# A window-attention and feed-forward kernel: score matmuls of the first two batches on tiles of 64 rows by 32 columns, and the second batch's value products in pieces of 32 moving columns

## The chip, the cores and the metric

The kernel runs on one core of one Trainium2 chip. The metric is the device time of one execution in microseconds (us): 975.45 us in the median of two runs (975.3 and 975.6). A profile of one execution lies beside it; its span is the time from the first to the last instruction.

The engines of a core are named in the profile as PE (TensorE matmul), PEld (its weight loads), DVE (VectorE), ACT (ScalarE), POOL (GpSimd) and SP (SyncE, which issues the DMAs).

## The reference

Eight batches, eight heads, 512 local and 32 global positions, head size 64. Local queries see the 32 global keys and the local keys within 32 positions; global queries see everything. The result goes through a feed-forward block.

```python
k_all = np.concatenate([k_g, k_l], axis=2)
s_g = scale * np.matmul(q_g, k_all.transpose(0, 1, 3, 2))
out_g = np.matmul(sm(s_g), v_all)
s_ll = np.where(np.abs(pos[:, None] - pos[None, :]) <= 32, scale * q_l @ k_l.T, -1e9)
s_lg = scale * np.matmul(q_l, k_g.transpose(0, 1, 3, 2))
a_l = sm(np.concatenate([s_lg, s_ll], axis=-1))
out_l = np.matmul(a_l, np.concatenate([v_g, v_l], axis=2))
x = np.concatenate([out_g, out_l], axis=2)  # to (4352 tokens, 512)
h = x @ w_in          # 512 -> 2048
y = (h - np.tanh(h)) @ w_out
```

(Lines shortened; `sm` is the softmax, `scale` is 1/8.)

## The kernel before

**Heads and pairs.** Two heads of a batch make a `Pair`: the even head lies in partitions 0 to 63 (`a.e` = 0), the odd one in 64 to 127 (`a.e` = 64). Four pairs make a batch. The 512 local queries of a head are four blocks of 128, taken two at a time (`tp` = 0, 1); a pair is thus visited twice for its scores, twice for its transposes and twice for its products.

**Scores** (`Pair.scores`, matmul on L1149). For a visit, each of the two heads has one PSUM bank with two blocks of scores. One matmul takes 64 rows (the head's 64 partitions), a stationary operand of 128 queries and a moving operand of `KC` = 224 keys. In the first two batches (`split` is false) the operands are plain fp32 and a visit is four matmuls: two blocks by two heads. In the later batches (`split` is true) the operands are split in a high and a low part (fp32r) and a visit is 12 matmuls. One plain fp32 matmul of the program shows in the trace as two weight loads and two matmuls; so a visit of the first two batches is 8 matmuls in the trace.

**After the scores** DVE adds the mask and takes the maximum (L1458), ACT the exponential (L1465), DVE the inverse sum (L1221, L1222), POOL normalises (L1228), PE transposes the probabilities (`Pair.transposes`, L1170: 16 matmuls of 64 rows and up to 128 stationary columns, moving 64), and ACT or DVE copy them to `keys_first` (L869).

**Products** (`Pair.add_product`, matmul on L1247). The stationary operand is 64 columns of values (128 or 96 rows), the moving one 160, 128, 96 or 64 columns of `keys_first`; the even head writes PSUM partitions 0 to 63, the odd one 64 to 127. `PARTS` has four parts for each of the two products of a pair, and their moving widths add up to 512 columns. So a product is 4 parts by 2 heads, 8 matmuls in the program and 16 in the trace, in every batch. Copies to `x_hi` (L869) and `x_lo` (L1258) follow.

**Feed-forward.** `Chunk.add_hidden` (L1520, input weights) and `Chunk.add_out` (L1568, output weights) run with one batch's delay: 128x512 matmuls of fp32r in three passes. Those of batch 0 begin near 58 us and share PE with the attention of batch 1.

**Fill.** Before 72 us of the planner's clock, dummy matmuls on a mask (L1814) are put where the planner sees PE waiting.

**Order.** Nothing is scheduled on the chip. `Order.run` is a planner in the kernel's own code: each operation has a due time, an engine and an estimated length (`d`; 0.85 for a plain score visit, 1.05 for a product of the first two batches), and the planner writes out one fixed order for each engine. PSUM banks 0 to 3 are handed round among scores, transposes and products; 4 to 7 hold the output sums. A score visit's two banks are free again once DVE has read them.

Of the kernel before, what the change touches and what calls it, by code (L numbers as in the profile page):

```python
# [16 lines left out]
P = 128  # L17
D = 64
KC = 224
# [4 lines left out]
def f32(ap):  # L24
    return ap.bitcast(F32)


def view(ap, dims, off=0):

    return bass.AP(ap.tensor, ap.offset + off, [list(ap.ap[0])] + [list(d) for d in dims])  # L30
# [19 lines left out]
class Order:  # L50
# [14 lines left out]
    def add(self, eng, fn, due, r=(), w=(), res=(), alloc=(), free=(), lat=0.0, xfer=0.0, rows=1.0, ldw=0.107, tail=0.107, lock=False, mode="f", glue=None):  # L65
        o = Op()
        engs = [x + (0.0,) * (3 - len(x)) + (lock,) * (len(x) < 4) for x in (eng if isinstance(eng, list) else [eng])]
        o.eng = {x[0]: x[1:3] for x in engs}

        o.lock = {x[0] for x in engs if x[3] or x[0] == "P"}  # L70
        o.xfer, o.rows, o.ldw, o.tail, o.mode = xfer, rows, ldw, tail, mode
        o.fn, o.due, o.lat, o.alloc, o.free = fn, due, lat, alloc, free
        o.n, o.ready, o.succ, o.start, o.args, o.seq = 0, 0.0, {}, None, {}, len(self.ops)
        before = {}
        for k in tuple(r) + tuple(w) + tuple(res):
            if k in self.writer:
                before[id(self.writer[k])] = self.writer[k]
        for k in tuple(w) + tuple(res):
            for x in self.readers.get(k, ()):
                before[id(x)] = x  # L80
        for x in before.values():
            x.succ[id(o)] = o
            o.n += 1
        for k in r:
            self.readers.setdefault(k, []).append(o)
        for k in w:
            self.writer[k] = o
            self.readers[k] = []
        o.next = None
        if glue is not None:  # L90
            glue.next, o.args = o, glue.args
        self.ops.append(o)
        return o
# [111 lines left out]
def kernel(ctx, tc, q_l, k_l, v_l, q_g, k_g, v_g, w_in, w_out, out):  # L205
    nc = tc.nc
# [45 lines left out]
    first_kw = cp.tile([P, 2, 2 * S], F32, name="first_kw", tag="x_lo1")  # L252
    first_kw = [first_kw[:, 0, :2 * KG], first_kw[:, 1, :2 * KG], first_kw2]
    first_q = cp.tile([P, 4 * DM], F32, name="first_q", tag="w_out_lo4")
    wide = [wpair, first_q[:, 2 * DM:].rearrange("p (n k) -> p n k", k=2), stage[:, 0], stage[:, 1]]
    first_q = [first_q[:, :S], first_q[:, S:2 * S], cp.tile([P, S], F32, name="first_q2", tag="hi0")]
    first_q = [x.rearrange("p (t c) -> p t c", t=NT) for x in first_q]
    keys_first = cp.tile([P, 2, 2, 2, 384], F32, name="keys_first", tag="kf")
    values = cp.tile([P, 2, 6, D], F32, name="values")
# [21 lines left out]
    def activations(b):  # L281
        return [t[0] if b % 2 == 0 else t[1]() for t in (x_hi, x_lo)]
# [10 lines left out]
    def bank(shape, j, dt=F32):  # L293
        n = 1
        for d in shape[1:]:
            n *= d
        t = banks[j][:shape[0], :n].bitcast(dt)
        if len(shape) == 3:
            t = t.rearrange("p (a c) -> p a c", a=shape[1])
        elif len(shape) == 4:  # L300
            t = t.rearrange("p (a c e) -> p a c e", a=shape[1], c=shape[2])
        return t
# [7 lines left out]
               step=102.1945, step1=21.2806, lag0=117.1894, hs0=56.6249, tol=0.0795, xs=0.0659, xw=9.5452, o_ld0=-439.2206,  # L310
# [557 lines left out]
    def copy(e, dst, src):  # L868
        (nc.scalar.copy if e == "A" else nc.vector.tensor_copy)(dst, src)  # L869

    def either(n, kind, psum=False):

        a, d = CFG.get("a_" + kind, 0.0), CFG.get("d_" + kind, CFG["pen"] if psum else 0.0)
        if psum:
            return [("A", (n + 190) / 1200, a), ("D", (n + 151) / 960, d)]
        return [("D", (n / 2 + 148) / 960, d, True), ("A", (n + 230) / 1200, a)]
# [95 lines left out]
    def keys_of(x, t):  # L972
        c = t // 2 * KG + t % 2 * P
        return x[:, c:c + KC]
# [33 lines left out]
    class Pair:  # L1008
# [123 lines left out]
        def scores(self, tp):  # L1132
            names = [(f"s{tp}", a.i) for a in self.heads]
            split = self.b > 1

            def mm(e, tags):
                t_ = [bank([P, 2, 256], tags[n]) for n in names]
                for a, x in zip(self.heads, t_):
                    setattr(a, f"s_{tp}", x)
                passes = [(0, 0), (0, 1), (1, 0)] if split else [(0, 0)]  # L1140
                for i in range(2):
                    for n, (qi, ki) in enumerate(passes):
                        for a, x in zip(self.heads, t_):
                            r, t = slice(a.e, a.e + D), 2 * tp + i
                            if split:
                                q, k = q_parts[qi]()[r, t * P:(t + 1) * P], keys_of(kw_parts[ki](), t)[r]
                            else:
                                q, k = first_q[self.set][r, t], keys_of(first_kw[self.set], t)[r]
                            nc.tensor.matmul(x[:, i, :KC], q, k, start=n == 0, stop=n == len(passes) - 1)  # L1149

            return dict(fn=mm, d=0.76 if split else 0.85, names=names, r=["kw0", "kl0", "kg0", "hk0", "lq"] if split else self.key[2:],
                        res=[a.p(tp) for a in self.heads], rows=0.8 if split else 1.0, ldw=0.107, tail=0.093 if split else 0.187)
# [83 lines left out]
        def add_product(self, pair):  # L1236
            o = ("o", self.j, pair, "p")
            cc, cols = self.jj, slice(256 * pair, 256 * pair + 256)
            x = [("x", self.b % 2, a.h, pair) for a in self.heads]
            over = [f"{n}{u}" for n in ("rk", "rq", "pw", "pk") for u in range(2)] if self.b == 1 else []  # L1240
            box = {}

            def mm(e, tags):
                box["o"] = bank([P, 288], tags[o])
                for i, (a, t, k, (c0, c1), o0) in enumerate(PARTS[pair]):
                    for h in self.heads:
                        nc.tensor.matmul(box["o"][h.e:h.e + D, o0:o0 + c1 - c0], values[:k, h.two, t + t // 2 + a], keys_first[:k, h.two, pair, a, c0:c1],  # L1247
                                         start=i == 0, stop=i == 3, skip_group_check=True)

            def places():  # L1250
                return [t[:, cc, cols].rearrange("p (t c) -> p t c", c=P) for t in activations(self.b)]

            def high(e, _):
                copy(e, places()[0], view(box["o"], [(160, 2), (1, P)]))

            def rest(e, _):
                src, g = box["o"], view(xg[:, cc, self.b // NG * P + self.b % NG:B * G], [(NG, G)])
                nc.vector.tensor_sub(places()[1], view(src, [(160, 2), (1, P)]), f32(places()[0]))  # L1258
                if pair:
                    nc.vector.tensor_add(g, src[:, P:P + G], g)  # L1260
                else:
                    nc.vector.tensor_copy(g, src[:, P:P + G])

            due = self.due(self.C["o_pv"] + self.C["o_pvp"] * pair)
            reads = [f"h{pair}0", f"h{pair}1", "hg0", "hg1", "vh0", "vh1"]
            add(("T", 0.92 if self.b > 1 else 1.05), mm, due, r=reads, w=[o], res=[k + (0,) for k in x] + over, alloc=[(o, self.tag)], rows=1.0,
                ldw=0.053, tail=0.135, mode="c")
            add(either(256, "ph", True), high, due + 0.5, r=[o], w=[k + (0,) for k in x])
            add(("D", 0.6), rest, due + 1, r=[o] + [k + (0,) for k in x],
                w=[k + (1,) for k in x] + [y for a in self.heads for y in (("xg", a.i, pair), ("xgw", a.i))], free=[(o, 1)])  # L1270
# [483 lines left out]
    for i in range(NH):  # L1754
# [6 lines left out]
        b, h = i // H, i % H  # L1761
# [89 lines left out]
```

## Time and profile before

| | before |
|---|---|
| time, median of 2 runs | 975.45 us (975.3 to 975.6) |
| span of the profiled execution | 973.7 us |
| PE busy | 960.3 us (99%) |
| DVE busy | 580.3 us (60%) |
| ACT busy | 452.1 us (46%) |
| POOL busy | 387.3 us (40%) |
| granted TensorE clock, mean | 1.000 |

Busy times of PE are those of pipelined matmuls with modelled ends: neighbouring matmuls overlap, so the pace of a block is read from start to start and not from the mean duration of one.

### The profile page before, as it was taken

Reading aid. Unit: us, or ns where it says so; the run is one execution under the profiler, and the core shown is the slowest. Engines: PE = TensorE matmul, PEld = TensorE weight load, DVE = VectorE, ACT = ScalarE, POOL = GpSimd, SP = SyncE. Lnnn points to the kernel's source line nnn. Section 1 sums busy time; section 2 is a strip of 40 time slices with the busy share of each in tenths; the row PEclk is TensorE's granted clock in tenths of the full one; section 3 lists DMA queues with packets and bytes.
Section 4 is the critical chain, followed back from the end, with each engine's and each line's share of the span. In section 5 each row is a group of like instructions: output and inputs, shape, how many; then the busy total and the mean of one; then the engine's idle time right before and its main releaser. Section 6 shows DMA issues by size and latency. Waiting matters only on the chain.

```text
span 973.7 us, 18494 instructions
## 1 busy us (share of the span) xinstructions
PE 960.3 (99%) x6453; PEld 784.5 (81%) x6453; DVE 580.3 (60%) x1907; ACT 452.1 (46%) x1275; POOL 387.3 (40%) x526
## 2 busy tenths in 40 slices
PE   8899999999999999999999999999999999999998
PEld 5677877888888888888888888888888888888897
DVE  6997667766657555766676567657636544422211
ACT  6966575745455434654355444534535434111111
POOL 4666756534444433434234444333332332211221
PEclk9999999999999999999999999999999999999999
DMA  8565244321223121322123122221202200100010
GB/s 233 151 178 165 84 114 114 92 38 35 50 39 82 33 39 34 88 40 34 32 38 83 23 39 39 71 50 34 50 14 69 39 17 1 44 1 1 1 44 22
DMA packets 195166, 57.32 MB, mean 59 GB/s; under 512 B 179712, under 2 KB 188416, under 8 KB 195072
## 3 DMA queue, kind: packets, MB, share of 16 engines
q1 hardware_dynamic: 193728, 55.61, 24.1%
q8 instruction: 51, 0.84, 0.4%
q10 hardware_dynamic: 1344, 0.52, 0.2%
q14 instruction: 43, 0.35, 0.1%
HBM read 47.19 MB, written 8.91 MB: 58 GB/s over the span
## 4 chain that ended last, share of the span: by engine, by line
PE 93%; DVE 2%; ACT 2%; SPq 1%; issue 1%; DMA 1%; POOL 0%; POOLq 0%; DVEq 0%; ACTq 0%
PE bank L1520 39%; PE bank L1568 38%; PE bank L1247 6%; PE bank L1149 4%; PE bank L1170 4%; PE bank L1339 1%; SPq L1030 0%; PE bank L1046 0%; DMA wraw<-in_q_g_dram 0%; ACT t L1465 0%; ACT pg L1090 0%; POOL prob L1228 0%; DVE keys_first L869 0%; ACT prob L1465 0%; ACT keys_first L869 0%
## 5 line engine op out<-in xcount | busy, mean ns | idle before, releaser
L1537 POOL TENSOR_TENSOR glo<-t,ghi 128x512 fp32r<-128x512 f32 x107 | 139.1, 1301 | 328.9 <-PE bank L1568 130.0
L1528 ACT ACTIVATE t<-bank 128x512 f32<-128x512 f32 x136 | 81.3, 598 | 302.7 <-PE bank L1520 292.3
L1531 DVE TENSOR_TENSOR t<-bank,t 128x512 f32<-128x512 f32 x136 | 93.9, 691 | 202.5 <-ACT t L1528 201.8
L1228 POOL TENSOR_SCALAR prob<-prob,st 128x224 f32<-128x224 f32 x240 | 108.0, 468 | 143.3 <-DVE st L1222 124.9
L1568 PE MATMUL bank<-w_out_hi,ghi 128*128 128x512 f32 x544 | 152.7, 394 | 0.0
L1568 PE MATMUL bank<-w_out_hi,glo 128*128 128x512 f32 x544 | 151.5, 392 | 0.0
L1568 PE MATMUL bank<-w_out_lo,ghi 128*128 128x512 f32 x544 | 151.3, 392 | 0.0
L1520 PE MATMUL bank<-x_hi,w_in_hi 128*128 128x512 f32 x512 | 140.3, 397 | 0.3 <-DVE x_hi L869 0.3
L1520 PE MATMUL bank<-x_lo,w_in_hi 128*128 128x512 f32 x512 | 137.4, 390 | 0.0
L1520 PE MATMUL bank<-x_hi,w_in_lo 128*128 128x512 f32 x512 | 136.2, 390 | 0.0
L1465 ACT ACTIVATE prob<-prob,st 128x224 f32<-128x224 f32 x240 | 113.2, 475 | 14.9 <-DVE st L1458 13.7
L1458 DVE CUSTOM_DVE_ANT_0 prob<-bank,mask 128x224 f32<-128x224 f32 x240 | 80.8, 386 | 64.7 <-PE bank L1149 57.8
L1568 PEld LDWEIGHTS bank<-w_out_lo,ghi 128*128 128x128 f32 x544 | 101.1, 188 | 22.1 <-issue 1.0
L1568 PEld LDWEIGHTS bank<-w_out_hi,glo 128*128 128x128 f32 x544 | 101.0, 188 | 21.9 <-issue 0.7
L1568 PEld LDWEIGHTS bank<-w_out_hi,ghi 128*128 128x128 f32 x544 | 100.2, 188 | 22.2 <-issue 1.4
L1520 PEld LDWEIGHTS bank<-x_hi,w_in_hi 128*128 128x128 f32 x512 | 93.7, 188 | 24.7 <-issue 3.2
L1520 PEld LDWEIGHTS bank<-x_lo,w_in_hi 128*128 128x128 f32 x512 | 95.9, 188 | 20.2
L1520 PEld LDWEIGHTS bank<-x_hi,w_in_lo 128*128 128x128 f32 x512 | 95.7, 188 | 19.7
L869 ACT COPY keys_first<-bank 128x512 f32<-128x512 f32 (+2 forms) x150 | 69.9, 516 | 89.2 <-PE bank L1170 88.3
L1247 PE MATMUL bank<-keys_first,values 128*64 128x160 f32 (+3 forms) x1024 | 68.7, 276 | 2.2 <-DVE keys_first L869 1.1
L1247 PEld LDWEIGHTS bank<-keys_first,values 96*64 96x64 f32 (+1 forms) x1024 | 56.3, 136 | 9.5 <-ACT keys_first L869 2.9
L1381 DVE STREAM_TRANSPOSE gt<-pg 32x128 f32<-32x128 f32 x192 | 53.1, 276 | 10.2 <-POOL pg L1360 4.3
(164 smaller groups left out, 1222.9 us busy)
## 6 DMA issues: line engine op xcount, KB each, us to landing
values<-in_v_l_dram SPq DMA_DIRECT2D x128, 72.0 KB, 2.2
out_dram<-wpair SPq DMA_DIRECT2D x32, 256.0 KB, 2.0
rawkq<-in_k_l_dram SPq DMA_DIRECT2D x96, 64.0 KB, 2.3
rawkq<-in_q_l_dram SPq DMA_DIRECT2D x96, 64.0 KB, 2.2
values<-in_v_g_dram SPq DMA_DIRECT2D x64, 48.0 KB, 2.0
first_q<-in_moe_w_in_dram SPq DMA_DIRECT2D x6, 512.0 KB, 4.5
stage<-in_moe_w_out_dram SPq DMA_DIRECT2D x6, 512.0 KB, 4.0
stage<-in_moe_w_in_dram SPq DMA_DIRECT2D x6, 512.0 KB, 4.0
```

The lines of the kernel that those rows point to most:

```text
L869: (nc.scalar.copy if e == "A" else nc.vector.tensor_copy)(dst, src)
L1149: nc.tensor.matmul(x[:, i, :KC], q, k, start=n == 0, stop=n == len(passes) - 1)
L1228: nc.gpsimd.tensor_scalar(x, x, st[:, c:c + 1], 1.0, op0=ALU.mult, op1=ALU.mult)
L1247: nc.tensor.matmul(box["o"][h.e:h.e + D, o0:o0 + c1 - c0], values[:k, h.two, t + t // 2 + a], keys_first[:k, h.two, pair, a, c0:c1], start ...
L1381: nc.vector.transpose(gt[r, :c], view(src, [(P, c), (1, 32)], 32 * q))
L1458: nc.vector.tensor_tensor_reduce(out=self.pt(2 * tp + i)[:, :KC], in0=getattr(self, f"s_{tp}")[:, i, :KC], in1=masks[2 * tp + i], scale=-0 ...
L1465: nc.scalar.activation(x, x, AF.Exp, bias=col[:, c0 + i:c0 + i + 1], scale=-1.0, accum_out=col[:, 8 + tp + c0 + i:9 + tp + c0 + i])
L1520: nc.tensor.matmul(self.h[s][:, j * n:(j + 1) * n], w[:, cc, f * P:(f + 1) * P], self.x()[xi][:, cc, :n], start=part == 0 and cc == 0 and ...
L1528: nc.scalar.activation(tt_[q], self.h[s], AF.Tanh)
L1531: nc.vector.tensor_sub(tt_[q], self.h.pop(s), tt_[q])
L1537: eng[e].tensor_sub(gg[q][1], tt_[q], f32(gg[q][0]))
L1568: nc.tensor.matmul(self.acc[tt], g[:, j * self.n + tt * P:j * self.n + (tt + 1) * P], low_out(f) if wi else high_out(f), start=s == 0 and ...
```

## The change

In the first two batches a score visit's matmul of 128 stationary columns becomes four of 32 columns, each with its own tile position (`a.e`, `c`), row half `a.e` and column group `c` = 0, 32, 64, 96. The moving operand is the same 224 keys for each of the four. The order within a visit is block, column group, head. A visit is now 16 matmuls in the program, 32 in the trace. The later batches' scores are as before.

In batch 1 alone (`self.b == 1`) a product's moving operand is cut in pieces of 32 columns, each a matmul of its own with the same values as stationary operand. 512 columns are 16 pieces for each head: 32 matmuls in the program, 64 in the trace, where there were 8 and 16.

```diff
                             else:
                                 q, k = first_q[self.set][r, t], keys_of(first_kw[self.set], t)[r]
-                            nc.tensor.matmul(x[:, i, :KC], q, k, start=n == 0, stop=n == len(passes) - 1)
+                            if split:
+                                nc.tensor.matmul(x[:, i, :KC], q, k, start=n == 0, stop=n == len(passes) - 1)
+                    if not split:
+                        t = 2 * tp + i
+                        for c in range(0, P, 32):
+                            for a, x in zip(self.heads, t_):
+                                r = slice(a.e, a.e + D)
+                                nc.tensor.matmul(x[c:c + 32, i, :KC], first_q[self.set][r, t, c:c + 32], keys_of(first_kw[self.set], t)[r],
+                                                 start=True, stop=True, tile_position=(a.e, c), skip_group_check=True)
@@
                 for i, (a, t, k, (c0, c1), o0) in enumerate(PARTS[pair]):
-                    for h in self.heads:
-                        nc.tensor.matmul(box["o"][h.e:h.e + D, o0:o0 + c1 - c0], values[:k, h.two, t + t // 2 + a], keys_first[:k, h.two, pair, a, c0:c1],
-                                         start=i == 0, stop=i == 3, skip_group_check=True)
+                    step = 32 if self.b == 1 else 512
+                    for c in range(c0, c1, step):
+                        e, z = min(c + step, c1), o0 + c - c0
+                        for h in self.heads:
+                            nc.tensor.matmul(box["o"][h.e:h.e + D, z:z + e - c], values[:k, h.two, t + t // 2 + a], keys_first[:k, h.two, pair, a, c:e],
+                                             start=i == 0 and c == c0, stop=i == 3 and e == c1, skip_group_check=True)
```

The lengths that the planner is told stay, so its order stays: on DVE, ACT, POOL and SP every instruction stands where it stood, and on PE only the two kinds of block are longer. Line numbers behind L1149 move by 8 (transposes are L1178), those behind the product by 11 (feed-forward L1531 and L1579, fill L1825); scores are L1156, products L1258.

On PE, a score visit of batch 1 between two feed-forward blocks, before (the output sums of L1568 end, four score matmuls in banks 103 and 100, one for each head):

```order
L1568 MATMUL bank_104<-w_out_hi,glo_73 128x512
L1149 MATMUL bank_103<-first_kw_63,first_q_84 128x224
L1149 MATMUL bank_100<-first_kw_63,first_q_84 128x224
L1149 MATMUL bank_103<-first_kw_63,first_q_84 128x224
L1149 MATMUL bank_100<-first_kw_63,first_q_84 128x224
L1520 MATMUL bank_102<-x_hi_87,w_in_hi 128x512 x4
```

The same place with the change (the pair of rows of banks 103 and 100 stands eight times; the first and the last are shown):

```order
L1579 MATMUL bank_104<-w_out_hi,glo_73 128x512
L1156 MATMUL bank_103<-first_kw_63,first_q_84 32x224
L1156 MATMUL bank_100<-first_kw_63,first_q_84 32x224
...
L1156 MATMUL bank_103<-first_kw_63,first_q_84 32x224
L1156 MATMUL bank_100<-first_kw_63,first_q_84 32x224
L1531 MATMUL bank_102<-x_hi_87,w_in_hi 128x512 x4
```

Nothing moved around it: 16 rows with an output of 32 partitions stand in place of four with 128.

On PE, a product of batch 1 behind the transposes, before (the shape is output partitions by moving columns; x4 is two parts of two heads):

```order
L1170 MATMUL bank_103<-idr,prob_97 128x64
L1170 MATMUL bank_100<-idr,prob_97 128x64
L1247 MATMUL bank_102<-keys_first,values 64x160 x2
L1247 MATMUL bank_102<-keys_first,values 64x96 x4
L1247 MATMUL bank_102<-keys_first,values 64x160 x2
L1520 MATMUL bank_101<-x_hi_87,w_in_hi 128x512 x4
```

and with the change:

```order
L1178 MATMUL bank_103<-idr,prob_97 128x64
L1178 MATMUL bank_100<-idr,prob_97 128x64
L1258 MATMUL bank_102<-keys_first,values 64x32 x32
L1531 MATMUL bank_101<-x_hi_87,w_in_hi 128x512 x4
L1531 MATMUL bank_101<-x_lo_88,w_in_hi 128x512 x4
```

Again nothing around it moved; 32 matmuls of 32 moving columns stand where 8 wider ones stood.

## Rows read from the trace of the kernel before

**Rows 1.** The page: span, PE's busy line, and the chain's shares by engine.

```profile
span 973.7 us, 18494 instructions
PE 960.3 (99%) x6453; PEld 784.5 (81%) x6453; DVE 580.3 (60%) x1907; ACT 452.1 (46%) x1275; POOL 387.3 (40%) x526
...
PE 93%; DVE 2%; ACT 2%; SPq 1%; issue 1%; DMA 1%; POOL 0%; POOLq 0%; DVEq 0%; ACTq 0%
```

**Rows 2.** Busy us of each engine (instructions) in three stretches, PEclk, DMA.

```profile
core 0: us, PE busy (x) PEld busy (x) DVE busy (x) ACT busy (x) POOL busy (x), PEclk, DMA share, GB/s
12.00:62.00 50.00, 44.56 (x500) 33.80 (x499) 46.38 (x167) 42.35 (x138) 32.68 (x49) 1.00 0.68 188
62.00:176.00 114.00, 113.76 (x733) 88.58 (x734) 82.16 (x220) 71.93 (x187) 69.97 (x81) 1.00 0.45 123
176.00:974.00 798.00, 793.57 (x5184) 656.32 (x5184) 446.47 (x1489) 333.06 (x938) 279.86 (x376) 1.00 0.18 40
```

**Rows 3.** Chain that ended last, in order of time: start us, us, what.

```profile
9.22 3.36 DMA wraw<-in_q_g_dram
12.71 0.43 PE bank L992 x4
...
17.03 0.96 PE bank L1149 x8
...
20.09 0.56 DVE pg L1084
...
59.60 2.60 POOL prob L1228 x4
62.24 0.40 PE bank L1170 x6
```

**Rows 4.** PE by line and shape, 62 to 176 us: scores of plain fp32.

```profile
L1149 PE MATMUL bank<-first_kw,first_q 64*128 64x224 f32 x56 | 7.0, 370 | 0.0
```

**Rows 5.** Products (L1247) from 62 to 176 us: ns min/median/max, first and last start, forms.

```profile
L1247 PE MATMUL bank<-keys_first,values x128: 217/297/351, 68.5 to 174.8; 128*64 128x160 f32 x64, 96*64 96x96 f32 x32, 96*64 96x128 f32 x16, 96*64 96x64 f32 x16
```

**Rows 6.** PE timeline around a product: start us, us, instructions merged.

```profile
115.04 0.71 PE L1170 MATMUL bank<-idr,prob 64*128 64x64 f32 x16
115.68 1.10 PE L1247 MATMUL bank<-keys_first,values 128*64 128x160 f32 x16
116.71 1.19 PE L1520 MATMUL bank<-x_hi,w_in_hi 128*128 128x512 f32 x4
```

**Rows 7.** PE timeline around two score visits, 129 to 132 and 139 to 142 us.

```profile
130.53 1.03 PE L1149 MATMUL bank<-first_kw,first_q 64*128 64x224 f32 x8
131.49 0.73 PE L1520 MATMUL bank<-x_hi,w_in_hi 128*128 128x512 f32 x2
...
139.76 0.69 PE L1170 MATMUL bank<-idr,prob 64*128 64x64 f32 x16
140.28 0.98 PE L1149 MATMUL bank<-first_kw,first_q 64*128 64x224 f32 x8
141.19 0.66 PE L1046 MATMUL bank<-idr,rawkq 128*128 128x128 f32 x4
```

**Rows 8.** PE timeline, the first two matmuls of a score visit and of a product.

```profile
130.53 0.46 PE L1149 MATMUL bank<-first_kw,first_q 64*128 64x224 f32 x2
...
115.68 0.36 PE L1247 MATMUL bank<-keys_first,values 128*64 128x160 f32 x2
```

**Rows 9.** Weight loads of that product, same columns as the PE timeline.

```profile
115.68 0.80 PEld L1247 LDWEIGHTS bank<-keys_first,values 128*64 128x64 f32 x16
```

**Rows 10.** PE timeline before 62 us; in brackets the idle time ahead and its releaser.

```profile
7.43 3.35 PE L1149 MATMUL bank<-first_kw,first_q 64*128 64x224 f32 x16
...
44.56 2.57 PE L1814 MATMUL bank<-mask 128*128 128x224 bf16 x25
47.95 1.10 PE L1247 MATMUL bank<-keys_first,values 128*64 128x160 f32 x16 [0.82 <-DVE keys_first L869]
```

## The prediction

> **What bounds the kernel now.** I read the page first, for which engine is full: PE is busy 99% of the span, and the chain that ended last runs through PE for 93% of it [rows 1]. A mean over stages says little of a change in the first 176 us, so next came the busy times by stretch [rows 2]. From 62 us on PE is busy 113.76 of 114.00 us: there is no idle time that could swallow anything, and every microsecond added to a block on PE is a microsecond of the kernel. From 12 to 62 us it is another kernel: PE is busy 44.56 of 50.00, so 5.4 us are idle, and DVE has 46.38. Third came the chain in order of time [rows 3]: a DMA for the global queries ends at 12.6 us, PE carries the chain to 20.09, with one score visit on it (17.03), then DVE, ACT and POOL carry it, and PE takes it back for good at 62.24. Fourth, the timeline of PE before 62 us [rows 10]: 25 fill matmuls, then 0.82 us of waiting for a copy on DVE. There a slightly longer block on PE is paid from waiting time.
>
> So the question is how much longer the two changed blocks become, and how many of them lie behind 62 us. Of plain fp32 score matmuls 56 are there, 8 for a visit, so 7 of the 16 visits [rows 4]. Of product matmuls 128 are there, 16 for a product, so 8 products, the first at 68.5 us [rows 5]: all eight of batch 1, the only ones that are cut.
>
> **The products.** Today a product takes 1.03 us of PE, from 115.68 to the next block at 116.71 [rows 6]. Its 16 matmuls become 64, with 64 weight loads. The moving columns stay: 512 for each head. What is new is 48 more loads and 48 more starts, and each piece moves so little that its load may no longer hide. No row shows a load of 64 columns with 32 moving. The nearest row is the transposes: 64 stationary rows, few moving columns (64), a load of up to 128 columns for each, two tiles side by side. 16 of them take 0.52 us where the next block has the same tile shape (139.76 to 140.28 [rows 7]), 0.0325 us each with its load, and 0.64 us where the tile shape changes behind them (115.04 to 115.68 [rows 6]): 0.12 us for the change. With that pace a product takes 64 x 0.0325 + 0.12 = 2.20 us, 1.17 more, and eight of them 9.4 us.
>
> Bounds: below, nothing, if loads and starts stay hidden as now and only moving columns count. Above, a piece costs no more than today's wider matmul, 1.03 / 16 = 0.064 us: 64 x 0.064 = 4.1 us, 3.1 more, 25 us in all. I take 0.0325: like the transposes the pieces move little, and their loads have half the columns.
>
> **The scores.** Today's visit takes 0.96 us (130.53 to 131.49), or 0.91 behind transposes of the same tile shape (140.28 to 141.19) [rows 7]. Its first two matmuls, one for each row half, run at the same time: two of them in 0.46 us, where the mean one has 370 ns [rows 8, 4]. 8 matmuls become 32, each with the same 224 moving columns, but on eight tiles where there were two. If all eight stream side by side, four rounds are left for each tile as now, and then the starts count: 32 x 0.0325 + 0.12 = 1.16 us, some 0.25 more than the 0.91 to 0.96 of today. Seven visits: 1.8 us. Three of the seven follow transposes, whose tile shape is then no longer that of the scores: 3 x 0.12 = 0.4 us. Bounds: nothing at the low end (the loads are a quarter as wide); at the high end the column groups take turns, which is a rival below.
>
> Do column groups run side by side at all? The product says so for two: its two heads use the same rows and different halves of the columns, and its first two matmuls take 0.36 us together at a median of 297 ns for one [rows 8, 5]; its 16 loads are through in 0.80 us, under the matmuls [rows 9]. For four column groups on one row half no row speaks. The Trainium skill speaks against the change here: "TensorE: Matmul & The Clock Gate", Part 3, section "The mechanism", says that a weight load overlaps matmuls in flight only where its row group differs. By it neither the four column groups of a score nor the pieces of a product could hide a load, and the sum would be that of the rival on turns. The product of today has loads and matmuls of both heads on the same rows, and they overlap, so by this trace the rule is too strict.
>
> **Before 62 us** nine visits grow by some 0.25 us. The first two (16 matmuls from 7.43 us, 3.28 us long, twice the later pace) end before the DMA that the chain waits for, at 12.6 [rows 10, 3]: nothing. The one at 17.03 lies on the chain: 0.25, and 0.12 more for a shape change near it. The other six meet 5.4 us of idle PE [rows 2] and chains through DVE, ACT and POOL; I leave 0.3 us for them. Together 0.7. If the idle time were no cover, it would be 6 x 0.25 + 6 x 0.12, some 2 us.
>
> **Other engines.** Their orders are unchanged. A score visit that ends later hands its banks to DVE later; DVE is busy 82 of 114 us in that stretch [rows 2] and has room. Behind a longer product stand PE's feed-forward blocks, which don't need it; the copies to `x_hi` come 1.2 us later, and so does the PE block that reads them, by the same delay. No DMA is added.
>
> **Sum.** 9.4 + 1.8 + 0.4 + 0.7 = 12.3 us on a span of 973.7: 986.0. The median of the runs, 975.45, lies 1.75 above that span, which I take as what lies around it: 987.8, rounded to 988, 1.3% more.
>
> **Rivals.**
>
> *Turns (slower).* The four column groups on one row half stream one after the other, for want of a path for their moving operands. Then a visit has 16 rounds for each row half instead of four. Four rounds take 0.91 to 0.96 us, so 16 take some 3.7, 2.7 more. Seven visits behind 62 us: 19 us. Seven between 12 and 62: 19, less the 5.4 idle, 13.5. With 9.4 for the products 42 us: about 1017. For it: no row shows more than two tiles at a time. Against it: two column groups do overlap [rows 8]. It decides for "slower" once a visit grows by 1.3 us, which is half of full turns: 7 x 1.3 + 9.4 + 0.7 = 19.2 us.
>
> *Pieces at the old price (slower).* A piece of 32 columns costs today's 0.064 us, because loads and matmuls on one tile go in series. Products 25 us, scores and the rest 2.9: 28 us, about 1003. Against it: the transposes do load and matmul at half of that [rows 7].
>
> *Free (no change).* Starts and loads hide as today's do [rows 9], only moving columns count. Then the shape changes are left, and the time is 976. For it: the floor on starts has not been seen, 0.0325 us is the pace of loads twice as wide. Against it: a piece has a quarter of today's mean of 128 moving columns to hide a load under.
>
> *Faster* would need a gain where PE is full: the only one is narrower loads ahead of seven visits, 0.1 us each; no gain near 2%.
>
> **How the numbers follow.** The forecast's own range is 981 to 993: from starts a fifth quicker than the transposes' to some more load time in each piece (a product 0.7 to 1.7 us longer). I give it 0.62. Free: 0.12. A way between forecast and turns, with pairs of column groups side by side or pieces near 0.05 us, 993 to 997: 0.12. Turns: 0.09. Old price: 0.05. A range of 977 to 997 leaves out half of free and both slow ones, 0.2. A measurement of this kernel tells some 2%, 19.5 us, from no change, so forecast, free and the way between are the same by that: 0.85 with a little taken off; slower 0.14; faster 0.01.
>
> **What would show it.** Right: products of batch 1 near 2.2 us from start to start, score visits 1.1 to 1.3 us, PE still full behind 62 us, later blocks as long as before, and the whole difference there by 176 us. Wrong: score visits of 2 us or more (turns), products of 4 us (old price) or 1.0 (free); a lower granted clock than the 1.00 of all three stretches [rows 2], which would lengthen blocks that were not touched; new PE waits for DVE or POOL behind 62 us, which would mean that the later scores are no longer covered.

## The result and the profile after

The changed kernel takes 984.55 us in the median of two runs (984.42 and 984.68) where the kernel before took 975.45: ratio 1.0094, interval 1.0065 to 1.0123, 9.1 us more. By the 2% bound that is the same; the forecast was 988 and +12.3 us. The profiled execution has a span of 982.9 us, 9.2 more than before.

| | before | after |
|---|---|---|
| time, us | 975.45 | 984.55 |
| span of the profiled execution, us | 973.7 | 982.9 |
| PE busy, us | 960.3 | 968.8 |
| start of the first score visit behind 62 us | 63.70 | 65.11 |
| a product of batch 1, start to next block, us | 1.03 | 1.99 |
| a score visit between feed-forward blocks | 0.96 | 0.92 |

The page of the changed kernel, its span and busy times, to be read against [rows 1]:

```profile
span 982.9 us, 20030 instructions
PE 968.8 (99%) x7221; PEld 790.2 (80%) x7221; DVE 579.4 (59%) x1907; ACT 452.6 (46%) x1275; POOL 387.3 (39%) x526
...
PE 93%; DMA 2%; POOL 2%; DVE 1%; ACT 1%; issue 1%; SPq 0%; POOLq 0%; DVEq 0%; ACTq 0%
```

768 matmuls more, and PE is as full as it was. The stretches of the changed kernel (busy us of each engine with instructions, granted clock, DMA), against [rows 2]:

```profile
12.00:62.00 50.00, 44.84 (x656) 32.80 (x657) 43.96 (x167) 42.04 (x139) 30.93 (x48) 0.97 0.67 183
62.00:176.00 114.00, 113.41 (x1180) 89.25 (x1179) 79.06 (x208) 68.87 (x176) 68.07 (x78) 1.00 0.45 122
176.00:974.00 798.00, 797.60 (x5281) 659.61 (x5281) 450.41 (x1501) 336.41 (x946) 282.48 (x381) 1.00 0.18 40
```

Behind 62 us PE stays full and the clock at 1.00. From 12 to 62 us the mean granted clock is 0.97; where that comes from is told below.

The PE timeline of the changed kernel around a product, two score visits and the last product of batch 1 (start us, us, instructions merged), to be read against [rows 6, 7]:

```profile
65.11 0.99 PE L1156 MATMUL bank<-first_kw,first_q 64*32 64x224 f32 x32
...
118.42 0.71 PE L1178 MATMUL bank<-idr,prob 64*128 64x64 f32 x16
119.06 2.06 PE L1258 MATMUL bank<-keys_first,values 128*64 128x32 f32 x64
121.05 1.20 PE L1531 MATMUL bank<-x_hi,w_in_hi 128*128 128x512 f32 x4
...
135.81 0.99 PE L1156 MATMUL bank<-first_kw,first_q 64*32 64x224 f32 x32
136.73 0.50 PE L1531 MATMUL bank<-x_hi,w_in_hi 128*128 128x512 f32 x1
...
144.99 0.69 PE L1178 MATMUL bank<-idr,prob 64*128 64x64 f32 x16
145.61 0.99 PE L1156 MATMUL bank<-first_kw,first_q 64*32 64x224 f32 x32
146.53 0.66 PE L1046 MATMUL bank<-idr,rawkq 128*128 128x128 f32 x4
...
182.31 2.06 PE L1258 MATMUL bank<-keys_first,values 128*64 128x32 f32 x64
184.30 0.37 PE L1150 MATMUL bank<-kw,hi 64*128 64x224 f32 x2
```

Three readings. A product goes from 1.03 to 1.99 us (119.06 to 121.05): 0.96 more, eight times 7.7. A score visit with four times as many matmuls is not longer but 0.04 us shorter (135.81 to 136.73). Behind transposes it takes 0.92 (145.61 to 146.53) where it took 0.91, and the transposes ahead of it take 0.62 (144.99 to 145.61) where they took 0.52 [rows 7], since the tile shape now changes between them. Four visits of the one kind and three of the other are 4 x (-0.04) + 3 x 0.11 = +0.2 us. The first visit behind 62 us starts 1.4 us later. 7.7 + 0.2 + 1.4 = 9.3, the 9.2 of the spans.

The weight loads of that product and of that visit in the changed kernel, same columns:

```profile
119.06 1.95 PEld L1258 LDWEIGHTS bank<-keys_first,values 128*64 128x64 f32 x64
...
135.81 0.56 PEld L1156 LDWEIGHTS bank<-first_kw,first_q 64*32 64x32 f32 x32 [0.36 <-issue]
```

The loads of a product now last as long as its matmuls: 1.95 of 1.99 us, where 16 loads were through after 0.80 of 1.03 [rows 9]. Those of a score visit are through after 0.56 of 0.92. So the theory that the experiments test: on one tile a matmul costs its weight load, as far as its moving columns don't cover it (L); not its start (S), which is what the forecast had priced.

### The profile page after: what moved, and what is told of

Its sections match the earlier page's. It is cut to its first block, busy times and chain, and to the rows that moved or that the text cites. A ratio compares the mean times of both kernels' runs of the same rounds, so it can differ in the third digit from the quotient of the medians.

```text
span 982.9 us, 20030 instructions
## 1 busy us (share of the span) xinstructions
PE 968.8 (99%) x7221; PEld 790.2 (80%) x7221; DVE 579.4 (59%) x1907; ACT 452.6 (46%) x1275; POOL 387.3 (39%) x526
## 4 chain that ended last, share of the span: by engine, by line
PE 93%; DMA 2%; POOL 2%; DVE 1%; ACT 1%; issue 1%; SPq 0%; POOLq 0%; DVEq 0%; ACTq 0%
PE bank L1531 38%; PE bank L1579 38%; PE bank L1258 7%; PE bank L1178 3%; PE bank L1150 3%; PE bank L1350 1%; DMA stage<-in_moe_w_in_dram 1%; DMA wpair<-in_moe_w_out_dram 1%; PE bank L1156 1%; POOL prob L1236 1%; PE bank L1046 0%; POOL t L1236 0%; DMA first_raw<-in_k_l_dram 0%; POOL w_out_lo L952 0%; POOL w_in_lo L952 0%
## 5 line engine op out<-in xcount | busy, mean ns | idle before, releaser
L1579 PE MATMUL bank<-w_out_hi,ghi 128*128 128x512 f32 x544 | 152.6, 394 | 0.0
L1579 PE MATMUL bank<-w_out_hi,glo 128*128 128x512 f32 x544 | 151.3, 392 | 0.0
L1579 PE MATMUL bank<-w_out_lo,ghi 128*128 128x512 f32 x544 | 151.2, 392 | 0.0
L1531 PE MATMUL bank<-x_hi,w_in_hi 128*128 128x512 f32 x512 | 140.2, 396 | 0.0
L1531 PE MATMUL bank<-x_lo,w_in_hi 128*128 128x512 f32 x512 | 137.4, 390 | 0.0
L1531 PE MATMUL bank<-x_hi,w_in_lo 128*128 128x512 f32 x512 | 136.2, 390 | 0.0
L1579 PEld LDWEIGHTS bank<-w_out_lo,ghi 128*128 128x128 f32 x544 | 101.0, 188 | 22.2 <-issue 1.2
L1579 PEld LDWEIGHTS bank<-w_out_hi,glo 128*128 128x128 f32 x544 | 101.0, 188 | 21.8 <-issue 0.6
L1579 PEld LDWEIGHTS bank<-w_out_hi,ghi 128*128 128x128 f32 x544 | 100.2, 188 | 22.0 <-issue 1.0
L1531 PEld LDWEIGHTS bank<-x_hi,w_in_hi 128*128 128x128 f32 x512 | 93.6, 188 | 24.0 <-issue 2.8
L1531 PEld LDWEIGHTS bank<-x_lo,w_in_hi 128*128 128x128 f32 x512 | 95.8, 188 | 20.3
L1531 PEld LDWEIGHTS bank<-x_hi,w_in_lo 128*128 128x128 f32 x512 | 95.6, 188 | 19.8
L1258 PE MATMUL bank<-keys_first,values 128*64 128x160 f32 (+5 forms) x1408 | 75.5, 256 | 3.8 <-DVE keys_first L869 1.6
L1258 PEld LDWEIGHTS bank<-keys_first,values 128*64 128x64 f32 (+1 forms) x1408 | 65.4, 137 | 11.8 <-ACT keys_first L869 4.1
```

The source lines that it names most:

```text
L1258: nc.tensor.matmul(box["o"][h.e:h.e + D, z:z + e - c], values[:k, h.two, t + t // 2 + a], keys_first[:k, h.two, pair, a, c:e], start=i == ...
L1531: nc.tensor.matmul(self.h[s][:, j * n:(j + 1) * n], w[:, cc, f * P:(f + 1) * P], self.x()[xi][:, cc, :n], start=part == 0 and cc == 0 and ...
L1579: nc.tensor.matmul(self.acc[tt], g[:, j * self.n + tt * P:j * self.n + (tt + 1) * P], low_out(f) if wi else high_out(f), start=s == 0 and ...
```

## The experiments

**The parts apart.** First the score tiles alone: the second part of the change is undone (all diffs here stand against the changed kernel).

```diff
-                    step = 32 if self.b == 1 else 512
-                    for c in range(c0, c1, step):
-                        e, z = min(c + step, c1), o0 + c - c0
-                        for h in self.heads:
-                            nc.tensor.matmul(box["o"][h.e:h.e + D, z:z + e - c], values[:k, h.two, t + t // 2 + a], keys_first[:k, h.two, pair, a, c:e],
...
+                    for h in self.heads:
+                        nc.tensor.matmul(box["o"][h.e:h.e + D, o0:o0 + c1 - c0], values[:k, h.two, t + t // 2 + a], keys_first[:k, h.two, pair, a, c0:c1],
+                                         start=i == 0, stop=i == 3, skip_group_check=True)
```

> The scores of the first two batches on tiles of 64 rows by 32 columns, the products as before. Theory L (what a small matmul costs is the load of its weights, which hides as long as enough columns move on its tile): a score visit is no longer than before, some 0.92 us from start to start where it was 0.91 to 0.96, the seven visits behind 62 us give 0.0 to -0.3 us, and what is left is what happens before 62 us. Of that the changed kernel lost 1.4 us, 1.2 of it next to 3.4 us at half the granted clock from 51 us on; if the score tiles bring that fall of the clock, the time is 976.5 to 977.5 and the trace shows the fall again near 51 us; if it was chance, 975.2 to 975.8 and no fall. Theory S (each start of a matmul costs about 0.03 us, as I predicted): visits of 1.16 us, 2.5 us in all, 978.

Measured: 976.7 us against 975.61 on the same chip, ratio 1.0009 (1.0001 to 1.0018). Visits of 0.92 us, as in the changed kernel, so S is wrong on the scores. The profile shows no fall of the clock (its mean is 1.000), and all the same the first visit behind 62 us comes at 64.99:

```profile
64.99 0.99 PE L1156 MATMUL bank<-first_kw,first_q 64*32 64x224 f32 x32
65.90 1.20 PE L1528 MATMUL bank<-x_hi,w_in_hi 128*128 128x512 f32 x4
```

The executions whose mean granted clock is 1.000 say the same by themselves: six with the score tiles have a median of 976.8 us, eleven of the kernel before 975.5. So the loss before 62 us belongs in this run to the score tiles or to chance, and not to the clock.

Then the products alone: the first part is undone.

```diff
-                            if split:
-                                nc.tensor.matmul(x[:, i, :KC], q, k, start=n == 0, stop=n == len(passes) - 1)
-                    if not split:
...
+                            nc.tensor.matmul(x[:, i, :KC], q, k, start=n == 0, stop=n == len(passes) - 1)
```

> The products of the second batch in pieces of 32 moving columns, the scores as before. Both theories, from the blocks of the changed kernel (1.99 us from start to start against 1.03): 8 x 0.96 = 7.7 us, so 983.1. If the two parts of the change do not add up (a wait that each hides for the other), it is under 982.5 or over 984. No fall of the granted clock near 51 us if the score tiles bring it.

Measured: 983.5 us, ratio 1.0079 (1.0065 to 1.0092), +7.7 from the ratio and +7.9 from the medians, with products of 1.99 us (118.06 to 120.04, rounded). This part is as priced by its blocks. The first score visit behind 62 us starts at 63.81, nearly as before the change, but takes 1.28 us there instead of 0.96:

```profile
63.81 1.35 PE L1149 MATMUL bank<-first_kw,first_q 64*128 64x224 f32 x8
65.09 1.21 PE L1523 MATMUL bank<-x_hi,w_in_hi 128*128 128x512 f32 x4
...
118.06 2.06 PE L1250 MATMUL bank<-keys_first,values 128*64 128x32 f32 x64
120.04 1.20 PE L1523 MATMUL bank<-x_hi,w_in_hi 128*128 128x512 f32 x4
```

**What a small matmul costs: load or start.** In this kernel and the next two the scores are as in the kernel before. First the loads are made half as wide, with more matmuls than in the change:

```diff
-                    step = 32 if self.b == 1 else 512
+                    step = 64 if self.b == 1 else 512
+                    narrow = (0, 32) if self.b == 1 else (0,)
+                    w = 32 if self.b == 1 else D
...
-                        for h in self.heads:
-                            nc.tensor.matmul(box["o"][h.e:h.e + D, z:z + e - c], values[:k, h.two, t + t // 2 + a], keys_first[:k, h.two, pair, a, c:e],
+                        for p in narrow:
+                            for h in self.heads:
+                                nc.tensor.matmul(box["o"][h.e + p:h.e + p + w, z:z + e - c], values[:k, h.two, t + t // 2 + a, p:p + w], keys_first[:k, h.two, pair, a, c:e],
...
+                                                 **(dict(tile_position=(0, h.e + p)) if w == 32 else {}))
```

> Scores as before; the second batch's products in pieces of up to 64 moving columns, and the values loaded as two halves of 32 columns, each on its own column group (four in all). A product is then 72 or 80 matmuls in the trace, more than the 64 of the changed kernel, each with a load half as wide. Theory L: a load of 32 columns takes some 0.03 us and hides under 64 moving columns; the four column groups stream side by side, and a product takes 1.0 to 1.1 us from start to start as in the kernel before; time 975 to 977. Theory S (0.029 us for each start whatever is loaded): 72 to 80 starts take 2.1 to 2.3 us, products of 2.3 to 2.5 us, time 985 to 987. If four column groups take turns with these operands of 128 rows: over 2 us as well, but then with gaps of about 0.05 us between starts in groups of two.

Measured: 976.63 us (one run; 975.61 before). The PE timeline of a product in this kernel:

```profile
116.24 1.13 PE L1253 MATMUL bank<-keys_first,values 128*32 128x64 f32 x80
117.30 0.96 PE L1527 MATMUL bank<-x_hi,w_in_hi 128*128 128x512 f32 x3
```

Its weight loads:

```profile
116.24 1.02 PEld L1253 LDWEIGHTS bank<-keys_first,values 128*32 128x32 f32 x80
```

80 matmuls with 80 loads take 1.06 us (116.24 to 117.30), where 64 took 1.99. S, 2.3 to 2.5 us, is refuted; L, 1.0 to 1.1, holds. Four column groups over the same 128 rows stream side by side, loads included.

Then the loads of 64 columns again, with pieces of up to 64 moving columns:

```diff
-                    step = 32 if self.b == 1 else 512
+                    step = 64 if self.b == 1 else 512
```

> Scores as before; the second batch's products in pieces of up to 64 moving columns instead of 32, 40 or 36 matmuls in the trace, with the full load of 64 columns each. Theory L: a column group takes a new piece each 0.058 us, or as long as its columns move where that is longer (64 columns: about 0.053): 20 or 18 pieces for each head, 1.05 to 1.16 us from first to last start, 1.2 to 1.3 from start to start, 0.2 more than the 1.03 before; in all 1.5 to 2 us, 977 to 978. Theory C (a piece costs nothing until it moves fewer columns than 32): 1.03, 975.5 to 976.

Measured: 977.86 us (one run; 975.37 before), and a product of 1.28 us (117.20 to 118.48):

```profile
117.20 1.36 PE L1250 MATMUL bank<-keys_first,values 128*64 128x64 f32 x40
118.48 0.73 PE L1523 MATMUL bank<-x_hi,w_in_hi 128*128 128x512 f32 x2
```

Theory L gave 1.2 to 1.3. Half as many matmuls as in the kernel with narrow loads (40 against 80), and it takes longer. On each column group both kernels run the same 20 pieces one behind another, and both load as many columns in all (40 x 64 = 80 x 32); what differs is the width of a load on its group: what counts is that width. A fixed price for each start on a tile would make the two equal, and so would a single path on which the loads of all tiles follow one another: at the 0.029 us of the changed kernel for each load of 64 columns it would take 40 x 0.029 = 1.16 us in either, and 1.06 is less. The block prices 2 of the 2.5 us at most; this run's first visit behind 62 us was also 1.1 us late, with score matmuls of the old shape:

```profile
64.82 1.03 PE L1149 MATMUL bank<-first_kw,first_q 64*128 64x224 f32 x8
```

**Is PE full to the end?** The pieces of 32 columns in seven batches instead of one:

```diff
-                    step = 32 if self.b == 1 else 512
+                    step = 32 if self.b >= 1 else 512
```

> Scores as before; products in pieces of 32 moving columns in batches 1 to 7, 56 products instead of 8. Theory L with PE full from 62 us to the end: each product 0.96 us longer, 56 x 0.96 = 54 us, so 1029 to 1030, and the profile's PE share as before. If later batches have slack on PE that hides part of it: under 1025. If products of the later batches, two in a row, cost more than those of batch 1: over 1033.

Measured: 1031.01 us (one run; 975.37 before): 55.6 us for 56 products, 0.99 each, 1 us above the expectation. The stretches of this kernel:

```profile
62.00:180.00 118.00, 117.42 (x1042) 93.93 (x1039) 78.99 (x214) 70.39 (x182) 69.96 (x81) 1.00 0.43 119
180.00:1029.00 849.00, 844.59 (x7570) 710.79 (x7568) 448.98 (x1496) 336.62 (x943) 280.75 (x377) 1.00 0.17 38
```

A block lengthened anywhere behind 62 us is paid in full, in the late batches too.

**How far the starts of score tiles can be pushed.** Each 224 keys in two halves of 112, so 64 matmuls for a visit in the trace; the products are as in the kernel before:

```diff
-                                nc.tensor.matmul(x[c:c + 32, i, :KC], first_q[self.set][r, t, c:c + 32], keys_of(first_kw[self.set], t)[r],
-                                                 start=True, stop=True, tile_position=(a.e, c), skip_group_check=True)
+                                for m in (0, 112):
+                                    nc.tensor.matmul(x[c:c + 32, i, m:m + 112], first_q[self.set][r, t, c:c + 32], keys_of(first_kw[self.set], t)[r, m:m + 112],
+                                                     start=m == 0, stop=m > 0, tile_position=(a.e, c), skip_group_check=True)
```

> Products as before; score tiles of 64 rows by 32 columns as in the change, and each matmul's 224 keys in two halves of 112, so 64 starts for a visit instead of 32. Theory L: on a tile eight rounds of 112 columns, each longer than its load of 32 columns, stream like four of 224; a visit takes 0.9 to 1.0 us from start to start. Theory S: at the 0.02 us for a start that the changed kernel's visits allow at most (32 in 0.64 us), 64 starts take 1.28 us, and a visit 1.5 us; at 0.03 us, 2.2 us. Time 975 to 977 by L, 980 or more by S.

Measured: 981.96 us (one run; 975.61 before), and a visit of 1.30 us (135.69 to 136.99), between the two theories, so neither holds here as it stands:

```profile
135.69 1.37 PE L1157 MATMUL bank<-first_kw,first_q 64*32 64x112 f32 x64
136.99 0.73 PE L1529 MATMUL bank<-x_hi,w_in_hi 128*128 128x512 f32 x2
```

The visits don't make up the 6.4 us of this run: the seven behind 62 us, with the changes of shape, give some 2.8, while the first of them starts at 67.65, 4.0 later than before. Why the first 60 us lost so much here is not shown; the granted clock from 12 to 62 us was 0.97 in this profile, too.

In this order four matmuls in a row go to one tile (each of the program is two in the trace). The same 64 with the halves as the outer loop (this diff stands against the kernel just shown):

```diff
-                        for c in range(0, P, 32):
-                            for a, x in zip(self.heads, t_):
-                                for m in (0, 112):
+                        for m in (0, 112):
+                            for c in range(0, P, 32):
+                                for a, x in zip(self.heads, t_):
```

> The halved scores again (two matmuls of 112 keys for each of 224, tiles of 64 rows by 32 columns, products as before), but with the halves as the loop outside column groups and heads, so that at most two matmuls in a row go to one tile instead of four. With four in a row a visit took 1.30 us from start to start, where theory L gave 0.9 to 1.0 and theory S 1.5 or more. Theory Q (a tile that is still busy holds back those queued behind it): 0.90 to 1.05 us. Theory S', a price for each start with its load of about 0.017 us: 1.30 us again.

Measured: 977.85 us (one run; 975.1 before), and a visit of 1.01 us (132.78 to 133.79):

```profile
132.78 1.08 PE L1157 MATMUL bank<-first_kw,first_q 64*32 64x112 f32 x64
133.79 0.96 PE L1529 MATMUL bank<-x_hi,w_in_hi 128*128 128x512 f32 x3
```

The same matmuls and loads in another order are 0.29 us shorter: the order on the tiles held them back, not a price for each start. Theory Q's range holds it; that a busy tile holds back those behind it is the reading of that, and what it does in between is not seen. In this run the first visit behind 62 us starts at 65.58, so 1.9 of its 2.8 us lie ahead of that visit.

**Where the loss before 62 us belongs.** The score tiles in one batch alone; first in batch 0, then in batch 1:

```diff
-                            if split:
+                            if self.b != 0:
...
-                    if not split:
+                    if self.b == 0:
```

The second kernel has 1 in place of 0 in both lines; in both the products are as in the kernel before.

> Score tiles of 64 rows by 32 columns in batch 0 alone; batch 1's scores and all products as before. The score tiles of both batches cost 1.1 us in the median, and in their profile 1.3 us of it are there by 62 us, although each visit is as short as before. Theory T (tile shape): before 62 us transposes and scores of the same tile shape follow one another, and run into one another where one of them waits; with another shape each change costs some 0.12 us, so most of the loss comes from batch 0: 976.3 to 976.8. Theory N (noise of the DMAs in the first 60 us, not the tiles): 975.4 to 975.9, as the kernel before.

Measured: 976.65 us against 975.37, ratio 1.0012 (1.0003 to 1.0021).

> Score tiles of 64 rows by 32 columns in batch 1 alone; batch 0's scores and all products as before. Seven of these eight visits lie behind 62 us: four are 0.04 us shorter, three are 0.01 longer and cost 0.12 for the change of tile shape behind transposes, together +0.2 us. Theory T: 975.7 to 976.1. Theory N: the same, so this run and the one on batch 0 alone would both lie within 0.3 us of the kernel before, and not add up to the 1.1 us of both.

Measured: 976.08 us against 975.37, ratio 1.0009 (1.0000 to 1.0018). The first visits behind 62 us of the two kernels, batch 0 alone and then batch 1 alone:

```profile
64.41 1.03 PE L1150 MATMUL bank<-first_kw,first_q 64*128 64x224 f32 x8
```

```profile
63.64 0.99 PE L1156 MATMUL bank<-first_kw,first_q 64*32 64x224 f32 x32
```

Batch 0's run fits theory T, batch 1's lies at its upper end or above it, and 1.2 and 0.9 us don't add up to the 0.9 of both. The intervals are 1.8 us wide, so this comparison settles nothing. The profiles lean one way: with tiles in batch 0 the first visit behind 62 us starts at 64.41, 64.99, 65.11 and 65.81, and with halved keys at 65.58 and 67.65; without them at 63.64, 63.70, 63.81, 63.83, 64.18 (the pieces in seven batches) and 64.82. With one exception (64.82 against 64.41) every kernel with tiles in batch 0 is later than every kernel without, which chance alone would seldom give. How the tiles cost that time stays open. In one place of batch 0 where transposes and scores run into one another, the kernel before, from 27.74 to 31.54 us,

```profile
27.74 0.46 PE L1170 MATMUL bank<-idr,prob 64*128 64x64 f32 x7 [0.42 <-DVE st L1084]
...
29.33 0.35 PE L1149 MATMUL bank<-first_kw,first_q 64*128 64x224 f32 x1
29.33 0.40 PE L1170 MATMUL bank<-idr,prob 64*128 64x64 f32 x2
...
31.54 0.66 PE L1046 MATMUL bank<-idr,rawkq 128*128 128x128 f32 x4
```

takes 3.80 us, and the kernel with the score tiles alone, where they follow one another, 3.79:

```profile
27.85 0.46 PE L1178 MATMUL bank<-idr,prob 64*128 64x64 f32 x7 [0.42 <-DVE st L1084]
...
31.64 0.66 PE L1046 MATMUL bank<-idr,rawkq 128*128 128x128 f32 x4
```

So there the changes of tile shape, theory T's price, cost nothing on balance.

**The change again,** unchanged, beside the kernel before on one chip:

> The change as it is, beside the kernel before on one chip, to set it against the sum of its parts: scores alone gave +0.9 us (ratio 1.0009), products alone +7.7 (1.0079). If the parts add up: 8.0 to 9.5 us over the kernel before, ratio 1.0082 to 1.0097. If not: outside.

Measured: 984.66 us against 975.1, ratio 1.0097 (1.0080 to 1.0114). The parts, 1.0009 and 1.0079, give 1.0088: they add up within the intervals. This profile has the clock at full speed from 12 to 62 us:

```profile
12.00:62.00 50.00, 42.75 (x653) 31.37 (x654) 45.99 (x165) 42.76 (x139) 29.20 (x46) 1.00 0.65 182
```

Its PE timeline at the first score visit behind 62 us:

```profile
65.81 0.99 PE L1156 MATMUL bank<-first_kw,first_q 64*32 64x224 f32 x32
```

In the first profile of the changed kernel two stretches of 2 us show the fall:

```profile
51.00:53.00 2.00, 2.00 (x31) 1.88 (x32) 1.97 (x8) 1.58 (x7) 2.00 (x4) 0.52 0.21 42
53.00:55.00 2.00, 2.00 (x18) 1.40 (x16) 1.88 (x6) 1.18 (x3) 1.32 (x2) 0.63 0.55 126
```

That is mostly the lower level, 1.2 GHz, in these 4 us: (1 - 0.52) x 2 x 2 + (1 - 0.63) x 2 x 2 = 3.4 us of it, after PE had waited 0.5, 1.3 and 0.3 us between 44 and 51 us. The execution without the fall is no faster (span 983.4 against 982.9), and its first visit behind 62 us is later. So the fall doesn't explain the 9 us of the change; what such a fall costs, one pair of executions can't tell.

## Why the prediction was right, and where it was not

**Right.** PE full behind 62 us, with seven visits and eight products there, carried the whole argument, and the pieces in seven batches show it: 55.6 us for 56 products. Orders were unchanged, no new waits came up behind 62 us, the later blocks kept their length, and the difference is there by 184 us. The sign, the size within a third and the verdict "same" came out. One of the signs of being wrong showed, a granted clock below 1.00 (0.97 from 12 to 62 us), but the execution of the changed kernel with 1.00 there is no faster.

**The products: the right size, in part by luck.** Foretold 2.20 us for each, 9.4 in all; measured 1.99, 7.7. The transposes' 0.0325 us was the nearest row, and the pieces take 0.029: 64 starts spread over 2.06 - 0.22 = 1.84 us, 0.22 being the mean duration of the last. By the experiments that price is a load of 64 fp32 columns on one of two column groups, 0.058 us each. A product with loads of half that width, 80 of them, takes 0.03 us more than before the change; with 40 loads of the full width, 0.25. The forecast had said that a load may no longer hide under so few moving columns, and that is what happened. But its reason for this row ("like the transposes the pieces move little, and their loads have half the columns") should have made the pieces cheaper: the transposes take, on each of two tiles, a load of up to 128 columns every 2 x 0.0325 = 0.065 us, the pieces one of 64 every 0.058. That half the columns cost nearly as much in another kind of matmul was luck; no run here shows what sets the pace of the transposes.

**The scores: the step that failed.** "If all eight stream side by side, four rounds are left for each tile as now, and then the starts count." The first half is what happened: the visit's rounds are those of before, and it got 0.04 us shorter (its loads are a quarter as wide, which would fit; no run sets that apart). The second half is wrong: a start was priced like a transpose with its load. 32 starts lie within 0.99 - 0.355 = 0.64 us, 0.355 being the mean duration of one, and 80 starts of the kernel with narrow loads within 1.13 us: there is no price of 0.03 us for a start on another tile. 2.2 us foretold (1.8 for the visits, 0.4 for changes of shape), 0.2 measured; the changes of shape were there, at 0.10 us each for the 0.12 foretold.

**Before 62 us: too little.** 0.7 us foretold, 1.4 in the first profile; about 1 us by the runs with the score tiles alone. My ground, visits 0.25 us longer, is wrong, since they are not longer. That loss has no shown cause.

So the error of 3 us is 1.7 from the products and 2.0 from the scores, less 0.7 the other way.

**The rivals.** Turns is refuted by the visits of 0.92 us. So is the rule weighed there: the Trainium skill, "TensorE: Matmul & The Clock Gate", Part 3, section "The mechanism", lets a weight load overlap matmuls in flight only where the row group differs (the same section also lets one into a background weight buffer run ahead). By the first of these the loads of the four column groups of the kernel with narrow loads, all over the same rows, could not run under each other's matmuls; its 80 loads run for 1.02 of the 1.06 us of a product, under matmuls all along, so the trace disagrees with the "only". Old price is refuted by 1.99 us against 4.1. Free was true for the scores, and for the products only with loads half as wide.

## What to carry to other kernels

In this kernel cutting a matmul in smaller ones on separate tiles cost next to nothing as long as each still moved enough columns to cover its own weight load; cutting the moving side alone made the load the pace. So price a small matmul by the load on its tile against its moving time, and the count of starts low: 32 starts more in a score visit came to 0.09 us (1.01 against 0.92). Interleave the tiles in program order: the same 64 matmuls took 1.30 us with four in a row on a tile and 1.01 with two.

## What the runs showed of the hardware

Eight tiles of 64 rows by 32 columns, and four of 128 by 32, run side by side with plain fp32 operands: 32 matmuls of 224 moving columns in a visit of 0.92 us, 80 of up to 64 in a product of 1.06. 64 starts with their loads went within 1.08 us including the last one's run. The Trainium skill, "TensorE: Matmul & The Clock Gate", section "Wait — 56ns, not 53.3ns?", has a floor of about 25 ns from start to start, without a word there on tiles; an estimate by it is 1.6 us for these 64. Over several tiles the trace shows less, and the measurement decides.

Where PE is full, a change of tile shape between two blocks cost 0.10 us (transposes to scores, 0.62 against 0.52).

The profile with 3.4 us at the lower clock and the one without differ by 0.5 us, the first being the shorter. That such a fall costs nothing is not shown by it: of the 43 executions of the kernel before that ran beside the experiments, the three with the lowest mean clock (0.997 and 0.998) took 976.5, 977.0 and 978.4 us, the other 40 from 974.2 to 976.5, 975.4 in the median. Whether the clock made these longer or a wait lowered the clock, no run tells.
